# One order for the whole program in a scan and two-expert-layer kernel; the weights' low words shifted on another engine

## Chip, cores and metric

The kernel runs on one core of a Trainium2 chip. The metric is the device time of one execution in microseconds (us). A core has five engines that run side by side, each taking its own instructions strictly in order: PE (TensorE, matmuls), DVE (VectorE), ACT (ScalarE), POOL (GpSimd) and SP (SyncE, which here issues transfers). Transfers run on 16 DMA engines.

## What is computed

The reference is three layers in a row, all in float32 (cut to what matters; q, k, v and the decays a are [4, 8, 768, 48], the model has 384 columns and 3072 tokens):

```python
scale = np.minimum(mag, 0.999) / (mag + 1e-06)            # mag = |a|, a complex
for t in range(S):                                        # scan over 768 positions
    new_re, new_im = ar * S_re - ai * S_im, ar * S_im + ai * S_re
    S_re, S_im = new_re + k[t] v[t]^T, new_im
    y[t] = q[t] @ S_re
h = x @ w_in                                              # 384 -> 2048
x = (h * np.tanh(np.log1p(np.exp(h)))) @ w_out            # 2048 -> 384
e = argmax(x @ w_gate + modality_bias[modality_id])       # one of 8 experts
out[e's tokens] = gate_w * (np.maximum(x @ w1[e], 0) @ w2[e])   # 384 -> 1024 -> 384
```

`moe_w_in` and `moe_w_out` come as 64-bit floats; the kernel makes 32-bit floats of them.

## The kernel before

The 3072 tokens are worked in 12 units of 256. A 32-bit product is made of three matmuls on two rounded halves of each operand (high and low).

**Attention of a unit** has four parts. `att_lanes` (L345) normalises the decays and forms their running products: for unit 0 ACT takes squares of A into S (one instruction of 1536 elements), DVE adds, ACT takes Ln, Exp and Identity, DVE multiplies A, and a tree of products on DVE (S from A, A from S, down to `sn`, then up again into F) follows; its end is the mark D. `att_ends` scales q and k by F into X; `att_repack` sends X to QK by transfers from POOL and SP; `att_state` and `att_scores` make the state and the scores (tiles KT, pst, sc, ps, py) and store the result to `xT`. `moe1_x` loads it back as xr and splits it into xh and xl.

**First expert layer.** `moe1_weights` (L628) loads 16 weight tiles of 768 KB (eight of w_in, eight of w_out, names r) and decodes each in `decode` (L610): DVE shifts the low words right by 29 (TENSOR_SCALAR), DVE joins sign and low bits (SCALAR_TENSOR_TENSOR), ACT rescales the high words (Abs), DVE joins the two (SCALAR_TENSOR_TENSOR). Then ACT copies the high half to wt, two matmuls with the identity form the rest (tile pl), and ACT copies that. Each w_out tile also gets eight gate columns: PE transposes r (pt), ACT copies (wT), PE multiplies (pw). After that a unit takes 8 steps j: `moe1_h` (18 matmuls into ph), `moe1_act` (ACT five times over u and ph, and gh; DVE once for u and once for gl), and `moe1_o` (12 matmuls into po), which stands LAG = 3 steps after its h.

**Second expert layer.** Two routes (L945, one block of small DVE instructions with a few matmuls each, tiles pr and tb) sort the tokens of the first and of the second half by expert: first a table of experts per tile (etab), then a table of rows (tt). Tokens are worked in 15 tiles: 5 of the first half, 7 of the second, each of 256 rows, and 3 small ones of 128. A tile reads its expert's number into a register of SP, loads four 768 KB pieces of the expert's weights (r1s, r2s), splits each (ACT to v, DVE the rest to v), gathers its rows of x2 by an indirect transfer of POOL (xgs), transposes them (pts) and splits them (y), does four h steps (qhs, ACT hhs, DVE hls) and four o steps (qos), and scatters its rows (oss, an indirect transfer).

**What sets the order.** Class `Plan` (L87) holds strands, each with a name, a due time and a list of operations with estimated costs. `run` takes, one after the other, the operation that can start soonest by those estimates, strands with the earlier due time first; the due times are ranks, and the result is the fixed order of every engine's instructions. `due(u, j)` is FIRST + (8u + j) STEP. In this kernel the plan covers everything through unit 10 and route 0 (L1371 to L1382). After that (`Direct`) unit 11's first layer and the whole second layer are written in program order and ordered by the framework's own scheduler: tile n+1 is prepared ahead of tile n's matmuls, and route 1 stands behind tile 0 with a raised priority.

## Time and profile before

| | |
|---|---|
| median of 3 runs (lowest to highest) | 976.74 us (973.46 to 977.66) |
| the profiled execution, its span | 976.46 us, 974.4 us |
| mean granted TensorE clock | 0.973 of full |
| PE busy, PE weight load | 875.1 us (90%), 829.1 us (85%) |
| DVE busy, ACT busy | 736.0 us (76%), 652.5 us (67%) |
| POOL busy | 165.1 us (17%) |
| moved by DMA | 128.22 MB, 132 GB/s on average |

Busy time is read against the span; an engine that is not busy waits for another engine, for a transfer, or has nothing to do. The chain of work that ended last, as the page gives it, has only the last scatter in it and tells nothing here. So the span is read by stages: in each window, how long PE was idle and at which clock it ran (PEclk, as a share of 2.4 GHz), and then, at each idle stretch, what ended it.

### The profile page before, as it was taken

To read this page: it belongs to the slowest core of one execution; us is meant where nothing else is said; L and a number is where in the kernel's file an instruction comes from. 1 tells how busy PE (TensorE), PEld (TensorE's weight loads), DVE (VectorE), ACT (ScalarE), POOL (GpSimd) and SP (SyncE) were. 2 spreads that over 40 slices of the span, in tenths; PEclk is the share of its full clock that TensorE was granted. 3 is DMA by queue.
4 is the path that set the end of the run, shared out by engine and by line. 5 is a ranking of instruction groups with operands and counts; after the bars stand their busy time and mean duration, and the time that the engine had idled before them with its cause. 6 is when DMAs were issued, how large, how long until landed. Compare 5 with 4: busy or idle time off the path is not lost. (4 is left out here: it accounts for less than half of the span.)

```text
span 974.4 us, 17436 instructions
## 1 busy us (share of the span) xinstructions
PE 875.1 (90%) x6401; PEld 829.1 (85%) x6401; DVE 736.0 (76%) x1530; ACT 652.5 (67%) x1072; POOL 165.1 (17%) x237
## 2 busy tenths in 40 slices
PE   0398899999999999998999999999748999999994
PEld 0267889999999989998999999999748999999973
DVE  4999888889898879898889897565786755565550
ACT  2477968787969786878697969577632455456551
POOL 1020201112111220112011112000130232312210
PEclk9989899999999999998999999999977999999998
DMA  9842232424343443243324242203962677766740
GB/s 301 334 99 81 66 90 79 119 79 118 93 104 94 103 130 83 74 106 105 107 79 109 63 104 69 60 27 122 297 215 65 172 253 235 227 219 196 230 148 6
DMA packets 102749, 128.22 MB, mean 132 GB/s; under 512 B 34601, under 2 KB 76599, under 8 KB 102656
## 3 DMA queue, kind: packets, MB, share of 16 engines
q1 hardware_dynamic: 89680, 89.00, 30.7%
q0 software_dynamic: 12976, 38.03, 12.9%
q8 instruction: 52, 0.85, 0.4%
q14 instruction: 41, 0.34, 0.1%
HBM read 93.74 MB, written 14.82 MB: 111 GB/s over the span
## 5 line engine op out<-in xcount | busy, mean ns | idle before, releaser
L248 ACT ACTIVATE u<-u 128x512 f32<-128x512 f32 x352 | 217.7, 629 | 5.9
L248 PE MATMUL po<-wt,gh 128*128 128x392 f32 x704 | 187.8, 348 | 0.0
L248 PE MATMUL ph<-xh,wt 128*128 128x256 f32 x1056 | 180.5, 291 | 4.7 <-ACT xh L248 4.7
L248 PEld LDWEIGHTS ph<-xh,wt 128*128 128x128 f32 x1056 | 152.5, 194 | 9.7 <-ACT xh L248 5.9
L248 PEld LDWEIGHTS po<-wt,gh 128*128 128x128 f32 x704 | 122.5, 188 | 3.2 <-issue 3.1
L248 PE MATMUL po<-wt,gl 128*128 128x392 f32 x352 | 119.7, 340 | 0.0
L1168 PE MATMUL qhs<-y,v 128*128 128x256 f32 x792 | 104.7, 285 | 1.9 <-ACT y L606 1.9
L248 POOL DMA_DIRECT2D QK<-X x120 | 65.4, 553 | 227.1 <-ACT xs L248 72.5
L1168 PEld LDWEIGHTS qhs<-y,v 128*128 128x128 f32 x792 | 101.4, 192 | 2.2 <-ACT y L606 2.2
L606 ACT ACTIVATE v<-r1s 128x1536 fp32r<-128x1536 f32 x30 | 44.6, 1488 | 80.5 <-PE qhs L1168 69.1
L248 PE MATMUL ph<-xl,wt 128*128 128x256 f32 x528 | 94.6, 289 | 2.4 <-DVE xl L248 2.2
L1182 PE MATMUL qos<-v,hhs 128*128 128x384 f32 x384 | 96.1, 341 | 0.0
L607 DVE TENSOR_TENSOR v<-r1s,v 128x1536 fp32r<-128x1536 f32 x30 | 52.6, 1755 | 43.8 <-ACT v L606 43.7
L607 DVE TENSOR_TENSOR v<-r2s,v 128x1536 fp32r<-128x1536 f32 x30 | 52.7, 1755 | 41.2 <-ACT v L606 40.9
L248 ACT ACTIVATE u<-ph 128x512 f32<-128x512 f32 x88 | 52.1, 592 | 46.0 <-PE ph L248 43.4
L248 PEld LDWEIGHTS ph<-xl,wt 128*128 128x128 f32 x528 | 77.2, 194 | 4.2 <-DVE xl L248 4.2
L248 DVE SCALAR_TENSOR_TENSOR u<-u,ph 128x512 f32<-128x512 f32 x88 | 60.1, 682 | 24.6 <-ACT u L248 24.3
L1182 PE MATMUL qos<-v,hls 128*128 128x384 f32 x192 | 62.0, 346 | 15.1 <-DVE hls L1173 15.1
L248 DVE TENSOR_TENSOR gl<-u,gh 128x512 fp32r<-128x512 f32 x88 | 60.3, 686 | 14.0 <-ACT gh L248 13.8
L248 ACT ACTIVATE gh<-u 128x512 fp32r<-128x512 f32 x88 | 55.1, 627 | 21.9 <-DVE u L248 21.9
L1182 PEld LDWEIGHTS qos<-v,hhs 128*128 128x128 f32 x384 | 67.8, 190 | 0.1
L248 PEld LDWEIGHTS po<-wt,gl 128*128 128x128 f32 x352 | 66.1, 188 | 0.4 <-DVE gl L248 0.4
(241 smaller groups left out, 1703.6 us busy)
## 6 DMA issues: line engine op xcount, KB each, us to landing
r1s<-in_w SPq DMA_DIRECT2D x30, 768.0 KB, 4.6
r2s<-in_w SPq DMA_DIRECT2D x30, 768.0 KB, 5.4
QK<-X POOLq DMA_DIRECT2D x72, 96.8 KB, 3.5
QK<-X SPq DMA_DIRECT2D x72, 96.8 KB, 3.3
r<-in_wi SPq DMA_DIRECT2D x8, 768.0 KB, 13.1
r<-in_wo SPq DMA_DIRECT2D x8, 768.0 KB, 11.8
X<-in_q POOLq DMA_DIRECT2D x12, 384.0 KB, 4.7
A<-in_ai POOLq DMA_DIRECT2D x12, 384.0 KB, 4.1
```

The lines of the kernel that those rows point to most:

```text
L248: self.plan.add(self.name, *cost[:2], lambda: real(*a, **k), *cost[2:])
L606: g.nc.scalar.activation(out=hi, in_=raw, func=AF.Copy)
L607: g.nc.vector.tensor_sub(lo, raw, hi.bitcast(F32))
L1168: nc.tensor.matmul(ph[:, a, :], wv[f // 4][:, k, f % 4 * 128:(f % 4 + 1) * 128], xv[:, k, :], start=n == 0, stop=n == 8)
L1182: nc.tensor.matmul(po[t][:, 0:DM], hv[:, a, t * 128:(t + 1) * 128], wv[f // 4][:, f % 4, :], start=f == 0 and n == 0, stop=f == NF2 - 1 an ...
```

## The change

1. **One plan for the whole program.** `run` can be called twice and goes on where it stopped. The first call covers everything through h step 4 of unit 11 (CUT); the second covers the rest of unit 11 and the second layer, whose tiles are now strands (classes Tile, TileStep, SmallStep) with due times of their own (TSTEP 4.3). One Line holds the PE order of all steps of both layers: the o steps stand three h steps behind across tiles as well (two within a tile before), with two empty places between unit 11 and tile 0. Route 1 becomes a strand due two steps into tile 0. Route 0 may start earlier. The four weight loads of a tile are chained, and the gathered rows use one buffer.
2. **Decode.** The shift of a low word moves to ACT: the word's top byte, read as uint8 at a stride of 8 bytes, times 1/32 minus 31/64, written as a 32-bit integer. Decoding is due at 20 + 5n instead of 40 + 4n. The first weight's load waits until the first unit's decays have been issued, and goes from second to eleventh on SP. Splits of gate columns and of w_in tiles wait for the previous tile's use.
3. **The first unit's norm** runs in two halves of 384 columns.
4. FIRST and STEP, and the due times of unit 2's lanes and ends and of state and scores, move by some us.

```diff
-FIRST, STEP = 70.0, 5.6
+CUT = 8 * 11 + 5
+FIRST, STEP = 75, 5.8
...
+        start = min(self.free.values())
+        for k, n in room.items():
+            self.room[k] = [start] * n
+        room, free, at, log, moved = self.room, self.free, self.at, self.log, self.moved
...
+    parts = [slice(0, 384), slice(384, 768)] if u == 0 else [slice(0, 768)]
+    for i, h in enumerate(parts):
+        A_.activation(out=N[:, :, h], in_=Af[:, :, h], func=AF.Square, accum_out=g.asum[:, u + i * NU:u + i * NU + 1])
+        V.scalar_tensor_tensor(out=m[:, h], in0=m[:, h], scalar=TINY, in1=r[:, h], op0=ALU.max, op1=ALU.add)
+    for h in parts:
+        A_.activation(out=m[:, h], in_=m[:, h], func=AF.Ln)
+        A_.activation(out=m[:, h], in_=m[:, h], func=AF.Exp, scale=-0.5)
+        A_.activation(out=r[:, h], in_=m[:, h], func=AF.Identity, scale=-0.999 * EPS, bias=0.999)
+    for h in parts:
+        V.scalar_tensor_tensor(out=m[:, h], in0=m[:, h], scalar=1.0 / 0.999, in1=r[:, h], op0=ALU.min, op1=ALU.mult)
+        V.tensor_mul(Af[:, :, h], Af[:, :, h], m[:, h].unsqueeze(1).to_broadcast([128, 2, h.stop - h.start]))
...
-        with p.strand(f"lanes {u}", {0: 5, 1: 45, 2: 90}.get(u, due(u) - 75)):
+        with p.strand(f"lanes {u}", {0: 5, 1: 45, 2: 100}.get(u, due(u) - 75)):
...
-            with p.strand(f"state {ci}", due(u) - 40 + 6 * c):
+            with p.strand(f"state {ci}", due(u) - 45 + 6 * c):
...
-    V.tensor_scalar(out=lw, in0=lw, scalar1=29, scalar2=None, op0=ALU.logical_shift_right)
+    A_.activation(out=lw, in_=top, func=AF.Copy, scale=1.0 / 32, bias=-31.0 / 64)
...
+            top = raw[:, 0:2 * a * b].bitcast(mybir.dt.uint8).rearrange("p (a b w) -> p a b w", a=a, w=8)[..., 3]
...
+            if n == 0:
+                p.wait("a0")
...
-        with p.strand(f"decode {n}", 40 + 4 * n):
+        with p.strand(f"decode {n}", 20 + 5 * n):
...
+                if not o:
+                    p.wait(f"turned{n - 1}")
...
-        with p.strand(f"gate {n}", 41 + 4 * n):
+        with p.strand(f"gate {n}", 21 + 5 * n):
...
+            p.wait(f"used{n - 1}")
...
+    def give(self, lo, hi):
+
+        for n in range(lo, hi):
+            swap = n < len(self.steps) and self.steps[n].swap
+            todo = [self.steps[n].first] if n < len(self.steps) else []
+            if 0 < n <= len(self.steps):
+                todo.append(self.steps[n - 1].middle)
+            if n >= LAG:
+                todo.insert(0 if swap else len(todo), self.steps[n - LAG].second)
...
+        with p.strand(f"expert {n}", self.due - 60):
+            p.wait(f"etab{self.gi}")
+            p.call("sync", 1.5, 0.1, lambda: e.append(expert(g, self.gi, slot)))
+            p.mark(f"e{n}")
...
+            with p.strand(f"load {n} {k}", self.due - 45 + 4 * k), p.behind(f"R{n}_{k}"):
+                p.wait(f"e{n}", *([f"loaded{4 * n + k - 1}"] if n + k else []))
+                p.take("r")
+                p.call("sync", 0.65, 1.8, lambda r=r, src=src: p.real.sync.dma_start(out=r.unsqueeze(1), in_=src()), 2.4)
...
+            with p.strand(f"split {n} {k}", self.due - 14 + 3.5 * k):
+                p.wait(f"R{n}_{k}")
+                if n == 1:
+                    p.wait(f"H{8 * NU - 8 + 2 * k + 1}")
+                elif n > 1:
+                    p.wait(*self.tiles[n - 2].done(k))
+                split(g, hi, lo, r)
...
+        xg = g.mx.tile([128, 2, DM], F32, tag="xr", name=f"xg{n}", bufs=1)
...
+        with p.strand(f"gather {n}", self.due - 30), p.behind(f"G{n}"):
+            p.wait(f"tt{self.gi}", *(f"x2_{b}" for b in range(nr // 128)), f"tu{n - 1}" if n else f"X{NU - 1}")
...
+        with p.strand(f"turn {n}", self.due - 12):
+            p.wait(f"G{n}")
...
-    moe1(g, range(NU - 1), xT, x2)
-    moe1_x(g, NU - 1, xT)
-    w0 = g.lane.tile([128, 2, 17, 48], F32, tag="F", name="w0")
-    with p.strand("route", due(NU)):
-        p.wait(f"out{NU // 2 - 1}_1", f"s{2 * NU - 2}")
-        route(g, ins, [w0.rearrange("p i a r -> p (i a r)")], 0, tab, g.aps, "ka")
+    steps = [Step(g, u, j, xT, x2) for u in range(NU) for j in range(NP)]
+    line = Line(g, steps)
+    line.give(0, CUT)
+    w0 = g.lane.tile([128, 2, 2, 384], F32, tag="S4", name="ar0")
+    with p.strand("route 0", due(10)):
+        p.wait(f"out{NU // 2 - 1}_1", f"D{NU - 1}")
+        route(g, ins, [w0.rearrange("p i j n -> p (i j n)")], 0, tab, g.aps, "ka", f"s{2 * NU - 2}")
     with tc.manual_schedule():
         p.run(h=3, A=2)
-    g.plan = Direct(g)
     actx.close()
-    tiles = [(0, i, 2) for i in range(NA)] + [(1, i, 2) for i in range(NB)] + [(1, i, 1) for i in range(NS)]
-
-    def prep(n):
-        gi, i, halves = tiles[n]
-        return moe2_in(g, ins, gi, i, expert(g, gi, i if halves == 2 else NFM + i), x2, tab, n, f"s{n}", halves)
-
     mctx = ExitStack()
     moe2_setup(g, mctx)
     moe2_sets(g)
-    ops = {0: prep(0)}
-    flags(g, g.const)
-    moe1(g, [NU - 1], xT, x2)
-    for n in range(len(tiles)):
-        if n + 1 < len(tiles):
-            ops[n + 1] = prep(n + 1)
-        (moe2_out if tiles[n][2] == 2 else moe2_small)(g, ops.pop(n), out, f"s{n}")
-        if n == 0:
-            with tc.high_priority(300):
-                route(g, ins, route_tiles(g, "r"), 1, tab, g.m2.ps, "rt")
-                more(g, g.const)
+    w1 = g.wts.tile([128, WP[1]], F32, tag="w9", name="ar1")
+    Tile.tiles = tiles = []
+    steps.extend([NoStep] * 2)
+    for n in range(NA + NB + NS):
+        gi, i, halves = (0, n, 2) if n < NA else (1, n - NA, 2) if n < NA + NB else (1, n - NA - NB, 1)
+        tiles.append(Tile(g, ins, n, gi, i, halves, x2, out))
+        steps.extend(tiles[-1].steps())
+    with p.strand("flags", due(NU - 1, 4)):
+        p.take("h")
+        flags(g, g.const)
+        p.give("h")
+        p.mark("flags")
+    with p.strand("route 1", due(NU) + 2 * TSTEP):
+        p.wait(f"out{NU - 1}_0", f"out{NU - 1}_1", "flags", "tt0")
+        route(g, ins, [w1], 1, tab, g.m2.ps, "rt")
+        more(g, g.const)
+    line.give(CUT, len(steps) + LAG)
+    with tc.manual_schedule():
+        p.run(h=3, r=3, pt=2, xs=2)
```

What `first`, `middle` and `second` of a tile issue is what `moe2_out`, `moe2_small` and `put` issued before: the same matmuls, copies and transfers.

**Place 1, the start on DVE.** First the row of instructions before (r are raw weights, S, A and sn belong to unit 0's lanes):

```order
1 L248 SCALAR_TENSOR_TENSOR S_0_126<-S_0_126 128x768
2 L248 TENSOR_SCALAR r_160<-r_160 128x768
3 L248 SCALAR_TENSOR_TENSOR r_160<-r_160 128x768
4 L248 SCALAR_TENSOR_TENSOR S_0_126<-S_0_126 128x768
5 L248 TENSOR_TENSOR A_124<-A_124,S_0_126 128x1536
6 L248 TENSOR_TENSOR S_0_126<-A_124 128x1536
7 L248 TENSOR_TENSOR A_124<-S_0_126 128x384 x2
8 L248 TENSOR_TENSOR S_0_126<-A_124 128x4x192
```

and now:

```order
1 L261 SCALAR_TENSOR_TENSOR S_0_126<-S_0_126 128x384 x2
2 L261 SCALAR_TENSOR_TENSOR r_164<-r_164 128x768 x2
3 L261 SCALAR_TENSOR_TENSOR S_0_126<-S_0_126 128x384
4 L261 TENSOR_TENSOR A_124<-A_124,S_0_126 128x2x384
5 L261 SCALAR_TENSOR_TENSOR r_173<-r_173 128x768
6 L261 SCALAR_TENSOR_TENSOR S_0_126<-S_0_126 128x384
7 L261 TENSOR_TENSOR A_124<-A_124,S_0_126 128x2x384
8 L261 SCALAR_TENSOR_TENSOR r_173<-r_173 128x768
9 L261 TENSOR_TENSOR S_0_126<-A_124 128x1536
10 L261 SCALAR_TENSOR_TENSOR r_177<-r_177 128x768
11 L261 TENSOR_TENSOR A_124<-S_0_126 128x384 x2
12 L261 TENSOR_TENSOR S_0_126<-A_124 128x4x192
```

Decode instructions of three weights now stand inside the tree of products, where one stood before, and the shifts are gone from this engine.

**Place 2, the end of unit 11 on ACT.** Before (u and gh belong to unit 11's steps 5 to 7, v to tile 0's weights):

```order
716 L773 ACTIVATE u_6_7510<-u_6_7510 128x512
717 L774 ACTIVATE u_6_7510<-u_6_7510 128x512
718 L606 ACTIVATE gh_5_7470<-u_5_7468 128x512
719 L775 ACTIVATE u_6_7510<-u_6_7510 128x512
720 L776 ACTIVATE u_6_7510<-u_6_7510 128x512
721 L606 ACTIVATE gh_6_7512<-u_6_7510 128x512
722 L772 ACTIVATE u_7_7552<-ph_7_7533 128x512
723 L773 ACTIVATE u_7_7552<-u_7_7552 128x512
724 L774 ACTIVATE u_7_7552<-u_7_7552 128x512
725 L775 ACTIVATE u_7_7552<-u_7_7552 128x512
726 L776 ACTIVATE u_7_7552<-u_7_7552 128x512
727 L606 ACTIVATE v_0_7195<-r1s_0_7247 128x1536
```

and now (r0s and r1s are tile 0's weights):

```order
713 L261 ACTIVATE u_5_7511<-ph_5_7510 128x512
714 L261 ACTIVATE v_0_7378<-r0s_0_7401 128x1536
715 L261 ACTIVATE u_4_1076<-u_4_1076 128x512
716 L261 ACTIVATE u_5_7511<-u_5_7511 128x512
717 L261 ACTIVATE v_4_7379<-r0s_1_7402 128x1536
718 L261 ACTIVATE u_4_1076<-u_4_1076 128x512
719 L261 ACTIVATE u_5_7511<-u_5_7511 128x512
720 L261 ACTIVATE v_8_7382<-r1s_0_7403 128x1536
721 L261 ACTIVATE u_5_7511<-u_5_7511 128x512
722 L261 ACTIVATE gh_4_1078<-u_4_1076 128x512
723 L261 ACTIVATE u_6_7515<-ph_6_7514 128x512
724 L261 ACTIVATE u_5_7511<-u_5_7511 128x512
```

The splits of the weights of tile 0, which began behind step 7's activations, now stand between the activations of steps 4 and 5; those of tile 1 follow in the same way up to step 7.

**Place 3, route 1 on DVE at the first tiles.** Before, the end of the block of route 1 with tile 1's first hls behind it (arr is the route's):

```order
1165 L1053 TENSOR_SCALAR arr_7818<-arr_7818 128x24
1166 L1054 TENSOR_SCALAR arr_7818<-arr_7818 128x24
1167 L1056 CAST arr_7817<-arr_7818 128x24
1168 L1055 CAST arr_7817<-arr_7818 128x24
1169 L1065 TENSOR_TENSOR arr_7817<-iota_p,arr_7817 128x256
1170 L1065 TENSOR_TENSOR arr_7818<-iota_p,arr_7817 128x256
1171 L1066 TENSOR_TENSOR arr_7817<-iota_t,arr_7817 128x76 x2
1172 L1067 TENSOR_TENSOR arr_7818<-arr_7817,ids 128x2x76
1173 L1067 TENSOR_TENSOR arr_7819<-arr_7817,ids 128x2x76
1174 L1173 SCALAR_TENSOR_TENSOR hls_0_8058<-qhs_0_8038,hhs_0_8057 128x512
```

and now, around tile 0's first steps (ar is the route's):

```order
1061 L261 TENSOR_REDUCE ar_7398<-logit 128x12
1062 L261 TENSOR_TENSOR v_14_7393<-r1s_1_7411,v_12_7391 128x1536
1063 L261 SCALAR_TENSOR_TENSOR hls_0_7526<-qhs_0_7524,hhs_0_7525 128x512
1064 L261 TENSOR_TENSOR ar_7398<-logit,ar_7398 128x96
1065 L261 TENSOR_TENSOR ar_7398<-ar_7398,iota_e 128x96
1066 L261 TENSOR_REDUCE ar_7398<-ar_7398 128x12
1067 L261 SCALAR_TENSOR_TENSOR hls_1_7529<-qhs_1_7527,hhs_1_7528 128x512
1068 L261 TENSOR_TENSOR oh<-iota_e,ar_7398 128x96
1069 L261 TENSOR_TENSOR ar_7398<-logit,ar_7398 128x96
1070 L261 TENSOR_SCALAR ar_7398<-ar_7398 128x96
1071 L261 TENSOR_TENSOR v_2_7380<-r0s_0_7415,v_0_7378 128x1536
```

Where some 70 instructions of route 1 stood ahead of one hls, they now stand singly between the hls and the splits of tiles 0 to 4. Between unit 1's step 4 and unit 10's step 3 the order of every engine is the same as before.

## Rows read from the trace of the kernel before

**Rows 1.** Stages by window: length, busy us (instructions) per engine, PEclk, DMA share, GB/s.
```profile
25.00:87.50 62.50, 44.75 (x257) 33.41 (x258) 59.65 (x138) 36.95 (x66) 7.12 (x12) 0.93 0.56 184
87.50:112.50 25.00, 19.56 (x117) 17.92 (x116) 21.84 (x31) 21.97 (x40) 6.08 (x12) 0.84 0.20 60
112.50:675.00 562.50, 551.23 (x4282) 526.76 (x4280) 466.31 (x1062) 442.91 (x782) 83.63 (x141) 0.99 0.33 89
675.00:700.00 25.00, 22.09 (x146) 20.68 (x145) 17.26 (x17) 16.14 (x18) 3.20 (x2) 1.00 0.92 301
700.00:737.50 37.50, 17.01 (x100) 15.24 (x99) 30.16 (x110) 11.22 (x14) 8.69 (x8) 0.77 0.58 191
737.50:750.00 12.50, 12.50 (x81) 12.50 (x80) 9.14 (x20) 4.70 (x6) 0.00 (x0) 0.87 0.20 63
750.00:925.00 175.00, 175.00 (x1261) 174.66 (x1261) 104.89 (x125) 94.90 (x117) 46.27 (x37) 1.00 0.68 218
925.00:962.50 37.50, 32.95 (x171) 27.89 (x169) 15.54 (x15) 17.23 (x24) 5.07 (x5) 1.00 0.31 99
```

**Rows 2.** Timeline of PE, 24 to 110 us: start, duration, what, [idle before <-releaser].
```profile
83.76 0.62 PE L248 MATMUL ph<-xh,wt 128*128 128x256 f32 x3 [0.35 <-ACT xh L248]
...
100.97 0.92 PE L248 MATMUL pt<-ident,r 128*128 128x128 f32 x3 [5.41 <-ACT wT L248]
```

**Rows 3.** Timeline of DVE, 10 to 50 us: F's last products, q and k scaled.
```profile
36.15 1.03 DVE L248 TENSOR_TENSOR F<-S 128x384 f32<-128x384 f32 x2
...
44.83 3.82 DVE L248 TENSOR_TENSOR X<-F,X 128x768 f32<-128x768 f32 x4
```

**Rows 4.** Groups by line: decode on DVE and ACT, and two ACT instructions of the lanes.
```profile
L248 DVE SCALAR_TENSOR_TENSOR r<-r 128x768 uint32<-128x768 uint32 x32 | 29.8, 950 | 0.3 <-ACT r L248 0.2
...
L248 DVE TENSOR_SCALAR r<-r 128x768 uint32<-128x768 uint32 x16 | 8.4, 559 | 0.0
...
L248 ACT ACTIVATE r<-r 128x768 f32<-128x768 f32 x16 | 14.5, 926 | 3.3 <-DVE r L248 3.3
...
L248 ACT ACTIVATE S<-S 128x768 f32<-128x768 f32 x36 | 30.3, 841 | 1.1 <-DVE S L248 1.0
...
L248 ACT ACTIVATE S<-A 128x1536 f32<-128x1536 f32 x12 | 17.7, 1475 | 7.8 <-DMA A<-in_ai 7.8
```

**Rows 5.** Timeline of PE, 75 to 84 us: pieces of the weights back to back.
```profile
75.58 1.50 PE L248 MATMUL pw<-wg,wT 128*128 128x8 f32 x12
76.94 0.92 PE L248 MATMUL pl<-r,ident 128*128 128x384 f32 x2
...
77.89 0.51 PE L248 MATMUL pt<-ident,r 128*128 128x128 f32 x3
78.23 0.84 PE L248 MATMUL pl<-r,ident 128*128 128x384 f32 x2
```

**Rows 6.** Groups by line on ACT: an activation, a weight split, a row split.
```profile
L248 ACT ACTIVATE u<-u 128x512 f32<-128x512 f32 x352 | 217.7, 629 | 5.9
...
L606 ACT ACTIVATE v<-r1s 128x1536 fp32r<-128x1536 f32 x30 | 44.6, 1488 | 80.5 <-PE qhs L1168 69.1 <-DMA r1s<-in_w 9.7 <-DMA tab<-tt 1.7
...
L606 ACT ACTIVATE y<-pts 128x384 fp32r<-128x384 f32 x25 | 11.2, 490 | 2.7 <-PE pts L1139 2.7
```

**Rows 7.** Timeline of PE from tile 0 to tile 2: three waits.
```profile
707.24 2.29 PE L1168 MATMUL qhs<-y,v 128*128 128x256 f32 x9 [1.92 <-ACT y L606]
...
720.08 1.01 PE L1139 MATMUL pts<-ident,xgs 128*128 128x128 f32 x6 [1.77 <-DMA xgs<-x,tt]
...
734.74 0.69 PE L1182 MATMUL qos<-v,hls 128*128 128x384 f32 x1 [13.64 <-DVE hls L1173]
```

**Rows 8.** Timeline of DVE: a split before route 1's block, and tile 1's hls behind it.
```profile
717.29 1.76 DVE L607 TENSOR_TENSOR v<-r1s,v 128x1536 fp32r<-128x1536 f32 x1
...
734.00 0.68 DVE L1173 SCALAR_TENSOR_TENSOR hls<-qhs,hhs 128x512 fp32r<-128x512 f32 x1
```

**Rows 9.** Waits of PE, 112 to 675 us: us in total, times, longest.
```profile
PE ph L248 <- ACT xh L248: 4.4, 2, 3.0
```

More of the change, by code (lines that the diff above doesn't have):

```diff
@@ L73, in give, with call @@
         pass
+    def call(self, eng, cost, lag, run, data=0.0):
+        run()
 class Op:
@@ L98, in __init__ @@
         self.key = None
+        self.free = {e: 0.0 for e in ENG}
+        self.moved = 0.0
+        self.at, self.room, self.log = {}, {}, []
         for e in ENG:
@@ L137, in mark, with call @@
         self.parts[key] = self.parts.get(key, 0) + 1
+    def call(self, eng, cost, lag, run, data=0.0):
+        self.add(eng, cost, lag, run, data)
     def add(self, eng, cost, lag, run, data=0.0):
@@ L154, in run @@
     def run(self, **room):
-        room = {k: [0.0] * n for k, n in room.items()}
-        free = {e: 0.0 for e in ENG}
-        moved = 0.0
-        at, seen, parts = {}, {}, dict(self.parts)
-        log = self.log = []
+        start = min(self.free.values())
+        for k, n in room.items():
+            self.room[k] = [start] * n
+        room, free, at, log, moved = self.room, self.free, self.at, self.log, self.moved
+        seen, parts = {}, dict(self.parts)
         def mark(k, t):
@@ L174, in run @@
             st.rank, st.name, st.ops, st.n = (due, i), name, ops, 0
-            st.issue = st.result = st.waited = 0.0
+            st.issue = st.result = st.waited = start
             st.eng = None
@@ L233, in run @@
             st.n += 1
-        self.at = at
+        self.moved = moved
+        self.strands, self.parts = [], {}
 class Queue:
@@ L251, in cost @@
     def cost(self, what, out, a, k):
-        n = math.prod(out.shape[1:])
+        n = math.prod((k["in_"] if what == "tensor_reduce" else out).shape[1:])
+        if "indirect" in what:
+            return 1.0, 2.0, 1.0
         if "dma" in what:
@@ L572, in attention @@
             att_lanes(g, ins, u)
-        with p.strand(f"ends {u}", {0: 8, 1: 55, 2: 100}.get(u, due(u) - 62)):
+        with p.strand(f"ends {u}", {0: 8, 1: 55, 2: 110}.get(u, due(u) - 62)):
             p.wait(f"D{u}")
@@ L589, in attention @@
                 att_state(g, ins, ci)
-            with p.strand(f"scores {ci}", due(u) - 38 + 6 * c):
+            with p.strand(f"scores {ci}", due(u) - 43 + 6 * c):
                 if ci:
@@ L739 @@
 LAG = 3
+TSTEP = 4.3
 def moe1_h(g, u, j):
@@ L846, in second, with moe1 @@
             for t in range(2):
-                with p.strand(f"out {u} {t}", due(u + 1) - 40):
-                    moe1_out(g, u, t, x2)
-    for n in range(len(steps) + LAG):
-        swap = n < len(steps) and steps[n][1] == 0
-        if n >= LAG and swap:
-            second(n - LAG)
-        if n < len(steps):
-            first(n)
-        if n >= LAG and not swap:
-            second(n - LAG)
+                with g.plan.strand(f"out {u} {t}", due(u + 1) - 40):
+                    moe1_out(g, u, t, self.x2)
+def moe1(g, units, xT, x2):
+    steps = [Step(g, u, j, xT, x2) for u in units for j in range(NP)]
+    Line(g, steps).give(0, len(steps) + LAG)
 HB = NT // 256
@@ L942, in route_space, with route @@
     g.tt = [c.tile([128, 3, n], I32, name=f"tt{i}") for i, n in enumerate(NHALF)]
-def route(g, ins, tiles, gi, tab, ps, tag):
+def route(g, ins, tiles, gi, tab, ps, tag, after=None):
     nc = g.nc
@@ L979, in route @@
     O = g.oh[:, 0:n, :]
+    if after:
+        g.plan.wait(after)
     pr = ps.tile([128, 2, n, E], F32, tag=tag, name=f"pr{gi}", bufs=1)
```

276 lines of the change are left out of this document (248 added, 28 removed).

## The prediction

> **What bounds the kernel now.** I read the stages first [rows 1]: they tell where PE, the engine with the most to do, stands idle. From 112.5 to 675 us it is busy 551.23 of 562.50 us at clock 0.99, from 750 to 925 us without a gap. What it loses lies at three places. At the start it does its first useful layer step at 83.76 us [rows 2]; DVE is busy 59.65 of the 62.50 us before 87.5, and PE is idle 5.44 us of the next 25 at clock 0.84 [rows 1]. Around the change of layers it is idle 2.91 + 20.49 = 23.4 us between 675 and 737.5, and runs at 0.77 and then 0.87 of its clock [rows 1]. At the end it is idle 4.55 us between 925 and 962.5 [rows 1]. Then I read what ends these waits. The long one is 13.64 us, for an hls of DVE [rows 7]; DVE was not waiting but worked off route 1 between a split at 717.29 and that hls at 734.00 [rows 8]. At 100.97 PE waits 5.41 us for ACT's copy wT [rows 2]. In the middle the only wait of size is 4.4 us in two pieces for xh [rows 9].
>
> **The change of layers.** What can be won is the idle 23.4 us and the clock's loss. The clock's loss, estimated as busy time by missing share, is 17.01 x 0.23 + 12.50 x 0.13 = 5.5 us [rows 1]. Together 28.9. What comes instead:
> - *Unit 11's end.* ACT now has the splits of tiles 0 and 1 between the activations (place 2). From step 4's first activation to step 7's gh it does four steps of six instructions at 0.63, six splits at 1.49 and four row splits at 0.49 [rows 6]: 15.1 + 8.9 + 2.0 = 26.0 us. Behind that come DVE's gl (as long as an hls, 0.68 [rows 8]) and the last o step. PE has three h and seven o steps to do in that time. A tile has 126 matmuls in four pairs of h and o, and 1261 take 175 us [rows 1], so a pair takes 4.37 and one step about 2.19: ten make 21.9, with four transposes at 0.34 (77.89 to 78.23 [rows 5]) 23.3. ACT's side is 26.0 + 0.7 + 2.2 = 28.9, so PE waits 5.6 us, and with the little that tile 0's first splits wait for their transfers I take 6.5. If PE hides part of it behind work that I put later, 4; if the weights are late, 10.
> - *Route 1.* Its 16.7 us on DVE (717.29 to 734.00 [rows 8]) now stand in pieces between the splits and hls of tiles 0 to 4 (place 3). Busy DVE there is 104.89 of 175 us without it [rows 1], 10.5 in a tile of 17.5; five tiles leave 35 us, so it fits. Its last step still feeds tile 5's gather, and only a few matmuls stand between the last tb and that tile's transposes. Bounds are 0 and 4 us, about twice the 1.77 that PE waited for a gather before [rows 7]; I take 2, near that row.
> - *Clock.* A wait of 6 us leaves some of it, 1 us of the 5.5 now lost.
> - *The rest.* The single gather buffer makes POOL's gather wait for the previous tile's transposes; POOL has a tile of 17.5 us for it, which hides it. The chained loads put SP's register reads ahead of a tile's weights: tile 4's stand behind route 1's etab, at the end of tile 1, and are needed two tiles later, so 0.
>
> Sum: 28.9 - 6.5 - 2 - 1 = 19.4 us gained, between 13 and 24.
>
> **The start.** *DVE* loses 16 shifts, 8.4 us, and ACT gets 16 conversions for them [rows 4]. No row has ACT read bytes. The nearest has the same 768 elements at the same stride, r<-r at 0.926; below stands 0.841 for 768 plain elements, above 1.475 for twice as many [rows 4]. I take 0.93: 14.8 us on ACT, and 23.6 at the upper end. *Earlier decoding* pulls decode instructions ahead of unit 0's chain. Nine joins of 0.95 [rows 4] now stand before F's end (place 1 shows the first six) where a shift and two joins stood: 8.6 - 2.5 = 6.1 us later than 37.2 [rows 3]. In the scaling of q and k, which ended at 48.65 [rows 3], six joins replace three and three shifts, 1.2 more. So the chain leaves that part 7.3 us late. But up to the first xl DVE has 26 joins to do, 24.7 us, where it had 19 and 11 shifts, 24.2: what was put ahead is missing later. If DVE sets the pace to the end, the first ph comes at 84.3; if the transfers of QK and the steps of the scores do, at 91.1. I take 88, since DVE was full there only in part. That is 4.2 lost. *PE* by then has done more: six pairs of pl at 0.95, four transposes at 0.34 and one and a half double pw at 1.36 [rows 5], 5.7 + 1.4 + 2.0 = 9.1 us which it need not do after it. *ACT* is busy 36.95 of the 62.50 us before 87.5 [rows 1] and gets 20 more decode instructions by the first xh, 18.5 us, some of them before that window; it fills up but is not over. After the first ph it has less left, so the wait of 5.41 [rows 2] shrinks by a part; I take nothing, since its place in the row changes. The first weight's load now waits for the decays; on SP nothing is queued behind it that was ahead, since nine loads pass it, and it lands last of them. Its first join stands in the tree on DVE, so where it is late the whole chain waits: 0 to 1.5 us, taken as 0. The new waits of a weight's copies for the previous tile's transposes only order what PE does in turn anyway: 0. The norm in halves lets DVE start half a square sooner, 0.7 of 1.475 [rows 4], and adds a small fixed cost per instruction: 0. Sum: 9.1 - 4.2 = 4.9, taken as 5; between -4 and +9.
>
> A rule of the Trainium skill speaks against this part. The row is the DVE shift at 0.559 and the like ACT instruction at 0.926 [rows 4]. The page "ScalarE: Activation LUTs", section "Rules for kernel authors", puts additions and multiplications on VectorE and not on ScalarE, which it calls slower per element for them. The rows agree in the direction, at 1.7 times. By the rule the start loses and the time is that of the first rival, 961; by the rows' sum it is 952.
>
> **The rest.** In the middle the order is the same on all engines, so the 4.4 us for xh [rows 9] stay; moved due times there change nothing. At the end the small tiles have the o steps three behind instead of two: 0.5 us of the 4.55, between -2 and 3. Resumed planning, marks and the earlier route 0 lie beside PE's work: 0, hidden by the gapless PE at 0.99.
>
> **Sum.** 19.4 + 5 + 0.5 = 24.9 us off the profiled 976.46 (span 974.4 and 2.1 around it), which stands 0.28 below the median; so 976.74 - 24.9 = 952 us.
>
> **Rivals.**
> - *ACT becomes the bound at the start.* The conversions cost 1.475 instead of 0.93, 8.8 us more on the engine that has least room there. For it: ACT has 21.97 of 25 us busy behind 87.5 [rows 1]. Against it: the stride is that of a row which costs 0.926. The start then gives 5 - 8.8 = -4 and the time is 961.
> - *The drain keeps half the gap.* Weights of two tiles must land within unit 11's end, at the 301 GB/s of before [rows 1]; where they don't, ACT's splits wait in their place ahead of activations, and PE with them. If the sum at the change of layers is 9 and not 19, 962. With the first rival too, 971.
> - *Slower: the fixed order makes PE wait at every tile's border.* The framework's order had no gap from 750 to 925 us [rows 1]. Now the turn, the row splits and the first h of a tile stand at fixed places, set by estimated costs; where a gather or a split is later than estimated, PE waits, and what is behind it cannot pass. Price: 1.77 for a gather and 1.92 for y [rows 7], 3.7 at each of 14 borders, 52 us, so 1004. It decides from 25 / 14 = 1.8 us per border. Against it: splits stand a tile ahead and DVE and ACT have a third of their time free.
> - *Better.* The first ph comes at 84.3, 3.7 sooner, and the wait of 5.41 goes: 943.
>
> **How the numbers follow.** The forecast has 0.55, with a range of its own of 944 to 960. ACT as bound has 0.15 (the rule above is in that), the half drain 0.12, both 0.05, the borders 0.07, the better case 0.06. The range reaches to 942 and 968: it takes in the forecast, the first two rivals and most of the better case and leaves out both together and the borders. Half a per cent of the time is 4.9 us, about what a measurement can tell from none, so faster means under 971.9. Faster: 0.55 + 0.15 + 0.12 + 0.06, less 0.01 for their tails, 0.87; within 0.5%: most of the fifth, and borders that cost 1.4 to 2.1 us, 0.06; slower: the borders at their price, 0.07.
>
> **What would show it.** In the trace of after: no idle stretch of PE over 5 us between 675 and 740, and route 1's instructions spread over four tiles; waits of 5 to 7 us in all for gl or gh in unit 11's last steps; first ph between 84 and 91 us, with more pl ahead of it; ACT's byte conversion near 0.93; PE gapless through tiles 1 to 11 but for one wait for the gather of tile 5; the two xh waits unchanged. I would be wrong if ACT's conversion is over 1.2 us, if SP's loads for tile 0 land after unit 11's step 6, or if every tile shows a wait for y or hls.

## The result and the profile after

The changed kernel takes 952.07 us (median of 4 runs, 951.5 to 953.77) against 977.2 (973.46 to 978.52), a ratio of 0.977 with a 95% interval of 0.974 to 0.980. The profiled execution took 951.5 us, its span 949.6. The forecast was 952.

The page's first part. PE and its weight loads do the same work as before in a span that is 24.8 us shorter; ACT has 16.3 us more to do and DVE 3.3 less:

```profile
PE 874.9 (92%) x6401; PEld 828.8 (87%) x6401; DVE 732.7 (77%) x1517; ACT 668.8 (70%) x1093; POOL 175.2 (18%) x237
```

Stages by window of the changed kernel, in the columns of [rows 1]:

```profile
25.00:87.50 62.50, 47.90 (x263) 34.97 (x264) 56.49 (x134) 48.03 (x85) 7.13 (x12) 0.89 0.55 180
87.50:112.50 25.00, 19.71 (x115) 15.90 (x114) 22.28 (x33) 21.57 (x40) 6.12 (x12) 0.86 0.24 71
112.50:650.00 537.50, 527.43 (x4141) 505.18 (x4140) 453.92 (x1044) 423.81 (x747) 83.84 (x141) 1.00 0.36 97
650.00:675.00 25.00, 21.97 (x144) 20.95 (x144) 14.72 (x16) 20.96 (x33) 7.04 (x4) 0.99 0.36 120
675.00:687.50 12.50, 10.35 (x48) 9.31 (x48) 8.72 (x12) 7.15 (x10) 1.25 (x1) 0.61 0.87 308
...
700.00:900.00 200.00, 198.90 (x1421) 197.25 (x1419) 138.07 (x223) 109.84 (x132) 59.24 (x43) 1.00 0.67 212
900.00:912.50 12.50, 9.07 (x43) 7.88 (x43) 4.68 (x4) 4.54 (x6) 0.00 (x0) 0.86 0.41 140
912.50:937.50 25.00, 22.81 (x129) 21.12 (x127) 10.29 (x9) 12.91 (x18) 5.68 (x5) 1.00 0.28 85
```

PE's idle time between 675 and 737.5, 23.4 us before, is gone from there; 3.03 us stand before 675 and 2.15 behind it. What is new is a clock of 0.61 in that window and 3.43 us of idle time at 900.

Two rows of ACT serve as a ruler in every trace: the splits xh of unit 1 and of unit 11. Before, then after:

```profile
156.05 0.85 ACT L248 ACTIVATE xh<-xr 128x768 fp32r<-128x768 f32 x1
...
636.66 0.83 ACT L248 ACTIVATE xh<-xr 128x768 fp32r<-128x768 f32 x1
```

```profile
150.82 0.83 ACT L261 ACTIVATE xh<-xr 128x768 fp32r<-128x768 f32 x1
...
629.66 0.83 ACT L261 ACTIVATE xh<-xr 128x768 fp32r<-128x768 f32 x1
```

They cut a span into a start, a middle and an end. The start took 156.1 us and takes 150.8; the middle 480.6 and 478.8; the end 337.7 (to 974.4) and 319.9 (to 949.6). So the 24.8 us are 5.2 + 1.8 + 17.8. In the middle PE does the layer steps in the same order in both kernels, but it is not the same work throughout: some 55 of DVE's small instructions for route 0 have moved into it from the end.

The starts: the first ph of PE, and its waits soon after it:

```profile
90.75 0.52 PE L261 MATMUL ph<-xh,wt 128*128 128x256 f32 x3
...
96.46 0.94 PE L261 MATMUL pl<-r,ident 128*128 128x384 f32 x2 [1.79 <-ACT wt L261]
...
98.36 0.92 PE L261 MATMUL pt<-ident,r 128*128 128x128 f32 x3 [0.79 <-DVE wt L261]
100.72 1.01 PE L261 MATMUL ph<-xh,wt 128*128 128x256 f32 x3 [1.45 <-ACT wt L261]
```

The first ph comes 7.0 us later than in [rows 2], and in place of the one wait of 5.41 for wT there are three of note, which come to 4.03. More of the weights' work is behind it by then.

The end of unit 11 on PE, and the two waits of PE that are left in the second layer (over 0.3 us):

```profile
659.28 0.62 PE L261 MATMUL ph<-xh,wt 128*128 128x256 f32 x3 [1.06 <-DVE bad L261]
671.74 0.63 PE L261 MATMUL po<-wt,gh 128*128 128x392 f32 x2 [0.72 <-ACT gh L261]
673.62 0.45 PE L261 MATMUL po<-wt,gl 128*128 128x392 f32 x1 [1.25 <-DVE gl L261]
677.84 1.02 PE L261 MATMUL po<-wt,gh 128*128 128x392 f32 x2 [1.30 <-ACT gh L261]
679.72 0.69 PE L261 MATMUL po<-wt,gl 128*128 128x392 f32 x1 [0.85 <-DVE gl L261]
```

```profile
766.55 1.03 PE L261 MATMUL pt<-ident,xg 128*128 128x128 f32 x6 [0.95 <-DMA xg<-x,tt]
...
903.52 0.88 PE L261 MATMUL pt<-ident,xg 128*128 128x128 f32 x3 [3.43 <-DMA xg<-x,tt]
```

The 13.64 us for hls [rows 7] are gone. Five waits at unit 11's end come to 5.18 us: 4.12 for gh and gl, and 1.06 for bad. The last is a flag that the strand `flags` makes; it takes one of the tiles that the h steps use, so an h step waits for it, and neither a split nor an activation on ACT is the cause. 0.95 us go to a gather of a large tile and 3.43 to one of a small tile.

### The profile page after: what moved, and what is told of

Read it like the earlier page. It is cut to its first block, busy times and chain, and to the rows that moved or that the text cites. A ratio compares the mean times of both kernels' runs of the same rounds, so it can differ in the third digit from the quotient of the medians.

```text
span 949.6 us, 17369 instructions
## 1 busy us (share of the span) xinstructions
PE 874.9 (92%) x6401; PEld 828.8 (87%) x6401; DVE 732.7 (77%) x1517; ACT 668.8 (70%) x1093; POOL 175.2 (18%) x237
## 4 chain that ended last, share of the span: by engine, by line
PE 46%; ACT 22%; issue 11%; DMA 9%; DVE 8%; POOL 2%; SPq 0%; ACTq 0%; POOLq 0%; DVEq 0%
PE ph L261 11%; PE po L261 10%; ACT u L261 9%; PE py L261 5%; PE ps L261 5%; DMA out<-oss,tt 5%; PE qhs L261 4%; ACT X L261 3%; ACT S L261 3%; PE pst L261 3%; PE qos L261 3%; PE pl L261 2%; DVE ar L261 1%; ACT gh L261 1%; ACT v L261 1%
## 5 line engine op out<-in xcount | busy, mean ns | idle before, releaser
L261 ACT ACTIVATE u<-u 128x512 f32<-128x512 f32 x384 | 237.8, 629 | 6.5
L261 PE MATMUL po<-wt,gh 128*128 128x392 f32 x768 | 206.7, 350 | 2.3 <-ACT gh L261 2.0
L261 PE MATMUL ph<-xh,wt 128*128 128x256 f32 x1152 | 193.5, 288 | 6.6 <-ACT xh L261 4.1
L261 PEld LDWEIGHTS ph<-xh,wt 128*128 128x128 f32 x1152 | 163.5, 191 | 11.5 <-ACT xh L261 4.8
L261 PEld LDWEIGHTS po<-wt,gh 128*128 128x128 f32 x768 | 135.2, 190 | 6.6 <-issue 2.9
L261 PE MATMUL po<-wt,gl 128*128 128x392 f32 x384 | 132.0, 344 | 2.1 <-DVE gl L261 2.1
L261 PE MATMUL qos<-v,hhs 128*128 128x384 f32 x432 | 111.8, 339 | 0.0
L261 POOL DMA_INDIRECT xg<-x,tt x27 | 42.3, 1568 | 167.5 <-PE pt L261 116.6
L261 PE MATMUL qos<-v,hls 128*128 128x384 f32 x216 | 72.6, 336 | 0.0
L261 ACT ACTIVATE hhs<-qhs 128x512 fp32r<-128x512 f32 x48 | 28.7, 599 | 59.2 <-PE qhs L261 58.2
```

The lines of the kernel that those rows point to most:

```text
L261: self.plan.add(self.name, *cost[:2], lambda: real(*a, **k), *cost[2:])
```

## The experiments

The table has all runs, with start, middle and end of the profiled execution by the ruler. Ratios are to the kernel before on the same chip.

| run | median us (lowest to highest) | ratio, 95% interval | start | middle | end |
|---|---|---|---|---|---|
| before | 977.2 (973.46 to 978.52) | | 156.1 | 480.6 | 337.7 |
| after | 952.07 (951.5 to 953.77) | 0.977 (0.974 to 0.980) | 150.8 | 478.8 | 319.9 |
| old_start | 956.81 (954.66 to 967.62) | 0.984 (0.978 to 0.991) | 156.3 | 480.4 | 316.1 |
| late_decode | 953.54 (948.3 to 958.73) | 0.978 (0.972 to 0.984) | 152.2 | 481.1 | 317.3 |
| shift_dve | 962.97 (956.85 to 966.01) | 0.985 (0.980 to 0.990) | 158.3 | 484.7 | 321.0 |
| route1_block | 960.4 (956.3 to 962.05) | 0.985 (0.981 to 0.989) | 150.6 | 478.9 | 324.9 |
| two_buffers | 947.54 (947.27 to 948.97) | 0.974 (0.972 to 0.975) | 153.1 | 480.1 | 312.3 |
| late_splits | 945.47 (941.45 to 947.75) | 0.971 (0.968 to 0.974) | 148.5 | 480.7 | 313.6 |
| both | 944.45 (943.38 to 947.67) | 0.971 (0.969 to 0.973) | 150.8 | 479.1 | 312.1 |
| whole_norm | 949.16 (one run) | | 148.2 | 479.6 | 319.6 |
| after_again | 953.14 (947.83 to 957.38) | 0.977 (0.973 to 0.981) | 152.4 | 479.3 | 320.1 |
| both_whole | 941.61 (939.63 to 944.52) | 0.966 (0.964 to 0.969) | 148.7 | 478.8 | 310.3 |
| both_whole_late | 964.2 (961.51 to 965.29) | 0.989 (0.986 to 0.992) | 156.1 | 495.1 | 311.2 |

Six of these start exactly as the changed kernel does (after, route1_block, two_buffers, late_splits, both, after_again): their starts lie between 148.5 and 153.1, 151.1 on average. So two starts of one order can differ by 4.6 us. Ends differ as much: old_start, whose end has the changed kernel's order, has 316.1, where after, after_again and whole_norm have 319.6 to 320.1.

**old_start: the start undone.**

```diff
-    A_.activation(out=lw, in_=top, func=AF.Copy, scale=1.0 / 32, bias=-31.0 / 64)
+    V.tensor_scalar(out=lw, in0=lw, scalar1=29, scalar2=None, op0=ALU.logical_shift_right)
...
-        with p.strand(f"decode {n}", 20 + 5 * n):
+        with p.strand(f"decode {n}", 40 + 4 * n):
...
-            if n == 0:
-                p.wait("a0")
...
-    parts = [slice(0, 384), slice(384, 768)] if u == 0 else [slice(0, 768)]
+    parts = [slice(0, 768)]
...
-FIRST, STEP = 75, 5.8
+FIRST, STEP = 70.0, 5.6
```

> The changed kernel with every edit of the start undone: shift on DVE, decoding due 40 + 4n, one norm of 768 columns, the first weight's load second on SP, the earlier due times. On PE, DVE and ACT the order up to the first units is that of the kernel before. My theory (start worth 5.16 us at 348.70 against 343.54 for the same ph): 957, between 955 and 959, first ph at 83 to 85 and a wait of about 5 us for wT near 101. Rival, the start is worth nothing and the whole gain comes from the plan at the change of layers: 952, within 1. Rival, the start is worth more than its 5 us because a later phase of the middle runs at full clock (before had 0.83 from 450 to 462.5): 959 to 961.

It took 956.81 us. PE's timeline in this run has the first ph and the wait for wT of the kernel before:

```profile
84.58 1.01 PE L261 MATMUL ph<-xh,wt 128*128 128x256 f32 x3 [0.60 <-ACT xh L261]
...
102.16 0.91 PE L261 MATMUL pt<-ident,r 128*128 128x128 f32 x3 [5.41 <-ACT wT L261]
```

Its start is 156.3, like 156.1 before and 5.2 more than the average of 151.1; the sum had 5. The two ratios' intervals still overlap, so the times alone would not tell the two kernels apart. Against the kernel before, this run has the one plan and nothing of the start: 956.81 against 976.58 on the same chip, 20 us (9 to 21 by the interval), and its end is 21.6 us shorter. So the plan alone is worth about the 19.4 that the sum had for the change of layers. The profiled execution differs by only 3.2 us from that of the changed kernel, since its end is 3.8 us shorter: PE waits there 1.70 us for the small tile's gather, not 3.43, and its clock stays at 1.00 behind that wait; some 1 us of it has no such reason.

**late_decode: the due times alone.**

```diff
-        with p.strand(f"decode {n}", 20 + 5 * n):
+        with p.strand(f"decode {n}", 40 + 4 * n):
...
-        with p.strand(f"gate {n}", 21 + 5 * n):
+        with p.strand(f"gate {n}", 41 + 4 * n):
```

> The changed kernel with decoding due at 40 + 4n and gates at 41 + 4n again, the shift still on ACT. My theory (the gain is PE work that is done before the first ph, about 9 us, against a first ph some us later): first ph earlier, at 80 to 84, but six fewer pairs of pl ahead of it; time 955 to 957. Rival, what pays is only that DVE has 16 shifts less: 952 or lower, down to 949.

It took 953.54 us, and the interval doesn't tell it from the changed kernel. The first ph came when the theory said, 7.8 us sooner than after:

```profile
82.95 0.61 PE L261 MATMUL ph<-xh,wt 128*128 128x256 f32 x3
...
91.01 0.62 PE L261 MATMUL ph<-xh,wt 128*128 128x256 f32 x3 [2.48 <-ACT wt L261]
```

But what was to be lost with it was not: PE does the weights' work later, and unit 1's xh is reached at 152.2, within the changed kernel's own range. So in this kernel the early due time, on which the sum's 9.1 - 4.2 us rested, is worth no more than two executions differ by. In another version it is worth more: see both_whole_late.

**shift_dve: the shift back on DVE, the early due times kept.**

```diff
-    A_.activation(out=lw, in_=top, func=AF.Copy, scale=1.0 / 32, bias=-31.0 / 64)
+    V.tensor_scalar(out=lw, in0=lw, scalar1=29, scalar2=None, op0=ALU.logical_shift_right)
```

> The changed kernel with the shift on DVE again (TENSOR_SCALAR, 0.559 us in the trace of before), the early due times kept. My theory (DVE sets the pace of the first unit's chain, ACT has room for 0.92 us pieces): 14 shifts, 7.8 us, stand on DVE ahead of the first xl, the first ph comes at 93 to 97, time 955 to 958. Rival, the direction of the rule in the Trainium skill, page ScalarE: Activation LUTs, section Rules for kernel authors (simple arithmetic belongs on VectorE, which is faster for it): ACT was the tight engine, and the time falls to 948 to 951. The numbers of both come from the two durations 0.559 and 0.922 us.

It took 962.97 us, more than the theory gave. The first ph is where it was expected:

```profile
95.41 0.62 PE L261 MATMUL ph<-xh,wt 128*128 128x256 f32 x3 [0.47 <-ACT wT L261]
```

The start is 158.3, 7.2 over the average, for 7.8 us of shifts (14 of 0.559) ahead of the first xl. Two other things differ as well: PE's granted clock from 25 to 87.5 us is 0.81, where the changed kernel had 0.89, and the plan comes to another order in the middle, which takes 484.7 us instead of 479 to 481. So how much of the 11 us between the medians is the shift's own is not shown. The direction of the rule from the Trainium skill (ScalarE: Activation LUTs, Rules for kernel authors), that such arithmetic belongs on VectorE, is not borne out in the time; that VectorE is the faster engine for it is, as the next rows show (the page gives its factor for bf16, which no run here has). Groups by line of ACT in the changed kernel, the byte conversion and the rescaling of the high words:

```profile
L261 ACT ACTIVATE r<-r 128x768 uint32<-128x768 uint8 x16 | 14.6, 922 | 3.6 <-DMA r<-in_wi 3.5 <-DMA r<-in_wo 0.2
L261 ACT ACTIVATE r<-r 128x768 f32<-128x768 f32 x16 | 14.4, 914 | 3.6 <-DVE r L261 3.6
```

ACT needs 0.922 us for what DVE did in 0.559, and with the early due times the exchange pays. That it pays because each shift stood in the chain on DVE is argued and not shown: both_whole_late has the shift on ACT and gains nothing at the start.

**route1_block: route 1 in one piece.**

```diff
-    with p.strand("route 1", due(NU) + 2 * TSTEP):
+    with p.strand("route 1", due(NU) - 200):
```

> The changed kernel with route 1 due far earlier, so that it takes DVE in one piece as soon as unit 11 is out: 56 of its instructions stand between the second and the third hls of tile 0. My theory (spreading route 1 is what removed the wait of 13.64 us): the block takes about 15 us of DVE, PE has some 9 to 11 us of matmuls it can do meanwhile with three PSUM tiles for h, so PE waits 4 to 7 us there and loses some clock behind it; time 956 to 961. Rival, the o steps that stand three behind cover the block and the gain came from the steps of unit 11 and tile 0 alone: 952, within 1.

It took 960.4 us. Up to unit 11 its trace is that of the changed kernel to 0.2 us, so the difference lies in the end alone, 5.0 us in the profiled execution (324.9 against 319.9). PE's longest wait there, and the window that holds it:

```profile
706.08 1.20 PE L261 MATMUL tb<-ar 128*128 128x114 f32 x4 [6.07 <-DVE ar L261]
```

```profile
700.00:712.50 12.50, 6.43 (x32) 6.42 (x32) 11.61 (x38) 0.60 (x1) 0.00 (x0) 0.73 0.06 4
```

PE waits 6.07 us for the route's instructions on DVE, and the clock falls to 0.73. The expectation named the hls as what PE would wait for; in the trace it is the first tb, which PE has to reach in its order. What the block costs came out as expected: spreading the route is worth 5 to 8 us with the rest of the plan in place.

**two_buffers: a second buffer for gathered rows.**

```diff
-        xg = g.mx.tile([128, 2, DM], F32, tag="xr", name=f"xg{n}", bufs=1)
+        xg = g.mx.tile([128, 2, DM], F32, tag=("xr", "xh")[n % 2] if n > 2 else "xr", name=f"xg{n}", bufs=1)
...
-            p.wait(f"tt{self.gi}", *(f"x2_{b}" for b in range(nr // 128)), f"tu{n - 1}" if n else f"X{NU - 1}")
+            p.wait(f"tt{self.gi}", *(f"x2_{b}" for b in range(nr // 128)), *([f"tu{n - 2 if n > 3 else n - 1}"] if n else [f"X{NU - 1}"]), *(["TH0_3"] if n == 3 else []))
```

> The changed kernel with two buffers for gathered rows from tile 3 on (the second in the place of the first layer's xh), so that a gather waits for the transposes of the tile before the last and not of the last. In the changed kernel PE waits 3.43 us at 903.52 for the gather of a small tile, and its clock is 0.83 from 900 to 910. My theory (the single buffer costs this: a small tile leaves a gather some 7 us, not 17.5): the wait is gone or under 0.5, time 947 to 950. Rival (POOL's own row, scatters ahead of the gather, holds it, not the buffer): wait of 1.5 to 3.5 us as now, time 951 to 953.

It took 947.54 us. These are all waits of PE over 0.1 us behind 640 us in this run; no gather is among them:

```profile
PE po L261 <- ACT gh L261: 2.9, 2, 2.2
PE po L261 <- DVE gl L261: 2.5, 2, 1.3
PE ph L261 <- DVE bad L261: 1.1, 1, 1.1
```

The single buffer, which the sum had at 0, cost the changed kernel 3 to 5 us: 4.5 between the medians, 3 by the ratios, whose intervals overlap a little. The rows of POOL show it at the last small tile, first in the changed kernel, then in this run:

```profile
895.42 0.98 POOL L261 DMA_INDIRECT out<-oss,tt  x1 [3.18 <-ACT y L261]
896.71 2.18 POOL L261 DMA_INDIRECT xg<-x,tt  x1 [0.30 <-issue]
```

```profile
888.66 1.05 POOL L261 DMA_INDIRECT xg<-x,tt  x1 [6.32 <-PE pt L261]
```

With one buffer the gather must follow the transposes of the tile before, and the plan put it behind a scatter on POOL; it starts at 896.71, and PE waits for it from 900.09. With two it starts 8 us sooner, ahead of the scatters. So the rival names what the gather stood behind, but with a second buffer the plan no longer puts it there. Tile 5's wait at 766.55 is not the buffer's. Its gather was released by route 1's table tt:

```profile
759.73 2.52 POOL L261 DMA_INDIRECT xg<-x,tt  x1 [7.27 <-DVE tt L261]
```

In two_buffers tt releases it too, at 761.25, and POOL has 1.04 us of work with it and not 2.52; why is not shown.

**late_splits: tile 1's splits behind unit 11's last activation.**

```diff
-                    p.wait(f"H{8 * NU - 8 + 2 * k + 1}")
+                    p.wait(f"H{8 * NU - 8 + 2 * k + 1}", f"gl{8 * NU - 1}")
```

> The changed kernel with tile 1's four weight splits held back until unit 11's last activations are done (in the changed kernel two of them stand between step 7's activations). My theory (ACT bounds unit 11's end: 1.30 and 0.72 us of wait for gh, 1.25 and 0.85 for gl, then a clock of 0.51 from 675 to 685): 3.0 us less on ACT ahead of step 7's gh, the second pair of waits is gone, the clock there 0.8 or more, time 946 to 949. Rival (it only moves the wait): the first h of tile 1 waits for v, as long as what was saved, time 951 to 953.

It took 945.47 us. The waits of PE behind 640 us for gathers, gl and gh, and the window behind unit 11:

```profile
PE pt L261 <- DMA xg<-x,tt: 3.5, 2, 3.3
PE po L261 <- DVE gl L261: 1.3, 1, 1.3
PE po L261 <- ACT gh L261: 1.2, 2, 0.7
```

```profile
675.00:687.50 12.50, 11.97 (x90) 11.37 (x89) 10.51 (x18) 9.02 (x11) 0.00 (x0) 1.00 0.83 281
```

The waits for gl and gh are 2.4 us (0.73, 1.25 and 0.43), where they were 4.12, and the clock from 675 to 687.5 is 1.00 and not 0.61. The gain is larger than the waits: 1.7 us of them, and 4.0 us of clock (10.35 x 0.39, an estimate from the window of the changed kernel) are close to the 6.3 us by which this run's end is shorter. The clock's part is the less certain one. The same window in after_again, which has the changed kernel's waits, and in two_buffers, whose waits for gh and gl come to 5.4 us:

```profile
675.00:687.50 12.50, 9.75 (x41) 8.90 (x42) 9.40 (x13) 8.72 (x12) 3.03 (x2) 0.73 0.86 277
```

```profile
675.00:687.50 12.50, 7.51 (x31) 6.53 (x32) 9.93 (x12) 9.16 (x14) 4.51 (x2) 0.86 0.74 236
```

No wait came in the splits' place at tile 1.

**both.** Both edits together.

> The changed kernel with two buffers for gathered rows and with tile 1's splits held back, both as in the runs by themselves. My theory (two places, 230 us apart, which do not touch each other): the gains add, 942 to 946, no wait over 1.5 us behind 650 us. Rival (either one is given back): 948 to 952.

944.45 us, as expected, though it is not the sum of both: the end is 312.1, where either alone has 312.3 and 313.6. One new wait, of tile 5's first h, appears:

```profile
769.45 3.14 PE L261 MATMUL qhs<-y,v 128*128 128x256 f32 x15 [1.23 <-DVE y L261]
```

**whole_norm: the norm in one piece.**

```diff
-    parts = [slice(0, 384), slice(384, 768)] if u == 0 else [slice(0, 768)]
+    parts = [slice(0, 768)]
```

> The changed kernel with the first unit's norm in one piece of 768 columns again. My theory (halves let DVE begin half a square sooner and cost nothing else): the first product of the tree, at 20.16 us, comes 0.5 to 1.5 us later, and so does the first ph, 91 to 92; time within 2 us of 952. Rival (the halves only add instructions): first product of the tree at 19 to 20.

The tree's first product on DVE, in this run and then in the changed kernel:

```profile
19.23 1.75 DVE L261 TENSOR_TENSOR S<-A 128x1536 f32<-128x1536 f32 x1
```

```profile
20.16 1.75 DVE L261 TENSOR_TENSOR S<-A 128x1536 f32<-128x1536 f32 x1
```

It comes 0.93 us sooner without the halves. Here the rival holds: the halves only add instructions in front of the tree. The first ph comes at 91.35 all the same, 0.6 us later, as the theory had it. The one time, 949.16, doesn't tell more.

**after_again.**

> The changed kernel itself once more, beside the next run on the same chip, to see how far its executions differ and to set the better version against it. My theory (what differs between executions is how the clock is granted in the first 450 us, 2 to 3 us): 949 to 954, the same waits at the same places: 1.06, 0.7, 1.25, about 1.3 and 0.85 at unit 11's end and over 3 us for a small tile's gather. Rival (the waits behind 650 us vary by themselves): one of these is gone or over 2 us longer.

953.14 us, from 947.83 to 957.38. The waits at unit 11's end were the same to 0.6 us, but not those for gathers, which are, for tile 5 and for the small tile:

```profile
767.90 0.55 PE L261 MATMUL pt<-ident,xg 128*128 128x128 f32 x3 [0.92 <-DMA xg<-x,tt]
770.84 0.55 PE L261 MATMUL pt<-ident,xg 128*128 128x128 f32 x3 [2.40 <-DMA xg<-x,tt]
...
899.62 0.55 PE L261 MATMUL pt<-ident,xg 128*128 128x128 f32 x3 [1.89 <-DMA xg<-x,tt]
```

So the rival is right for gathers: with one buffer they cost 4.4 us in one execution and 5.2 in another, at different places. Tile 5's 3.32 us of these are route 1's again (its gather starts at 761.11, released by tt); of the small tiles it is the second that waits here, and the third in the changed kernel.

**both_whole.**

> Two buffers for gathered rows and tile 1's splits held back, as in the run of both, and the first unit's norm in one piece. My theory (halves gain nothing: alone, one piece put the tree's first product 0.93 us sooner, and the first ph 0.6 us later): within 1.5 us of the run of both, 943 to 946. Rival (one piece is better, as the single time of 949.16 against 952.07 may say): 940 to 942.

941.61 us, the best version of the study. The intervals of this run and of both meet at 0.969 and go no further, so one piece is probably better here, by some 3 us, as the rival had it; its start of 148.7 is within the range of kernels with halves, so where the 3 us come from is not shown. Waits of PE over 1 us behind 640 us:

```profile
PE po L261 <- DVE gl L261: 1.3, 1, 1.3
PE qhs L261 <- DVE y L261: 1.2, 1, 1.2
PE po L261 <- ACT gh L261: 1.2, 2, 0.7
PE ph L261 <- DVE bad L261: 1.1, 1, 1.1
```

**both_whole_late: and the old due times.**

```diff
-        with p.strand(f"decode {n}", 20 + 5 * n):
+        with p.strand(f"decode {n}", 40 + 4 * n):
```

(and the gates' 41 + 4n)

> The run of both_whole (two gather buffers, tile 1's splits held back, the norm in one piece), and decoding due at 40 + 4n and gates at 41 + 4n as in the kernel before, the shift on ACT. It tells whether the earlier due time is worth anything once the shift is off DVE. My theory after the runs so far (the shift's move is the gain, the due time is not): within 2 us of 941.6, so 939 to 944, first ph at 82 to 84. Rival, the reason on record for the start (about 9 us of PE work done before the first ph): 945 to 948.

Neither: 964.2 us. The start is 156.1, where both_whole with the early due times has 148.7. So here the due time is worth 7.4 us at the start, and with the shift on ACT the start is no better than old_start's 156.3 with the shift on DVE: the theory, that the shift's move is the gain and the due time is not, fails in this version. The middle is 495.1, some 14 to 16 us more than in the kernels that keep the middle's order of before, or nearly so. Waits of PE in the middle:

```profile
PE ph L261 <- ACT xh L261: 13.4, 5, 5.7
PE ph L261 <- DVE xl L261: 4.7, 6, 1.3
```

PE waits 13.4 us for xh, three times the 4.4 of [rows 9]. The plan takes at every step what can start soonest; from another start it came to another order of the ten units. In late_decode and shift_dve the middle's order is another too, and costs 1 to 6 us.

## Why the prediction was right, point by point

The total was right to 0.1 us, and that close it is luck: single terms missed by up to 3 us in both directions, and executions of the changed kernel alone lie between 947.83 and 957.38. By the profiled executions:

| term | forecast | found |
|---|---|---|
| idle time and clock to be won from 675 to 750 | 28.9 | all gone from there |
| waits at unit 11's end | -6.5 | -5.18, of which -4.12 for gh and gl |
| tile 5's gather | -2 | -0.95 (-3.32 in after_again) |
| clock behind unit 11 | -1 | about -4.0 (about -2.6 in after_again) |
| the last tiles | +0.5 | about -1.9 (about +0.9 in after_again) |
| the start | +5 | +5.2 |
| the middle | 0 | +1.8 |

What was found adds up to 23.9 of the 24.8 us.

- **The change of layers: right in its mechanism.** PE waits at unit 11's end for gh, which ACT makes, and for the gl behind it. The sum's 6.5 was too much: 4.12, under the 5 to 7 that were to show it. The fifth wait, 1.06 for bad, was not foreseen. late_splits bears the mechanism out: less on ACT ahead of the last gh, shorter waits. Route 1 in pieces is what removed the long wait: route1_block brings 6.07 us of it back. (The 16.7 us given for it on DVE include a split of 1.76.) Tile 5's gather waits for route 1's last step, as forecast, 0.95 or 3.32 us for 2. *Mis-sized: the clock.* The sum left 1 us to it; the window behind the waits ran at 0.61, about 4.0 us (10.35 x 0.39), and in after_again at 0.73, about 2.6 (9.75 x 0.27).
- **The single gather buffer: wrong.** The step said that POOL has a tile of 17.5 us for a gather. That holds for large tiles. A small tile is shorter, and its gather was waited for 3.43 us, with a clock of 0.86 in that window, about 1.3 us (9.07 x 0.14); against that stand the waits at small tiles that the kernel before had, 0.88, 1.24 and 0.69, 2.81 us in all, and which are gone. Hence -1.9 in place of +0.5. In after_again the one such wait is 1.89 us at full clock, so the same sum gives +0.9. two_buffers shows the cause: without the single buffer no such wait is left.
- **The start: right in size, its reason not shown.** The sum said that DVE's work ahead of the first xl stays the same and that PE wins by having done more of the weights before it. PE had done more: 66 of the 96 matmuls of pl stand ahead of the first ph, where 48 did. But late_decode has 48 again and reaches unit 1 at the same time within the spread, so that reason does not hold there. The other reason, that the shift's move off DVE pays by itself, does not hold either: old_start and shift_dve, with the shift on DVE, are 5.2 and 7.2 us later, but both_whole_late, with the shift on ACT and the old due times, is 5.0 us later too. What the runs show is this: all eight kernels with the shift on ACT and the early due times start at 148.2 to 153.1; the four runs that lack one or both start at 152.2 to 158.3. Each edit also changes the order that the plan comes to, so what the single edits are worth stays open. The bound on the shift's price on ACT was taken well, 0.93 for a measured 0.922. The halves of the norm, taken as 0, don't help: the tree starts 0.93 us later.
- **The rivals.** ACT did not become the bound at the start (shift_dve is slower, not faster). The drain did not keep half of its gap. No wait at the tiles' borders: PE was busy 198.90 of 200 us from 700 to 900. The better case did not come, since the first ph came at 90.75, near its late end.
- **The middle.** The same order of layer steps, but 1.8 us less. The two waits for xh are there as before (4.1 us). The clock behind the second one differs: before, 437.5 to 450 ran at 0.89 and 450 to 462.5 at 0.83; now at 0.86 and 1.00. Busy time by missing share makes that 3.2 and 1.3 us, an estimate that would account for the whole difference. No run aimed at it; the middles of the kernels with nearly this order lie between 478.8 and 480.7, so it may be no more than how the clock was granted.
